# Query, key and value loads in pieces of two heads instead of four, one relu per piece

## The chip, the cores and the metric

The kernel runs on one core of one Trainium2 chip. The metric is the device time of one execution in microseconds (us), lower is better. A core has TensorE (PE, matrix products; PEld is its weight load), VectorE (DVE), ScalarE (ACT), GpSimd (POOL) and SyncE (SP). DMA engines move data between HBM and the core's memory; here GpSimd issues all loads, SyncE nearly all stores and all transposing DMAs.

## The reference

It is an attention without softmax, followed by a gated feed-forward block. There are 8 batches, 12 heads, 448 positions, 64 elements a head; 3584 tokens, a model width of 768 and a hidden width of 1536. All inputs and the output are float32.

```python
scores = scale * np.matmul(q, k.transpose(0, 1, 3, 2))
attn = np.maximum(scores, 0.0) ** 2 / S
attn_out = np.matmul(attn, v)
x = attn_out.transpose(0, 2, 1, 3).reshape(B * S, H * D)
g = x @ w_gate
gelu = 0.5 * g * (1.0 + erf(g * inv_sqrt2))
out = (gelu * (x @ w_val)) @ w_out
```

## The kernel before

All arithmetic on TensorE is in bf16; a load casts from float32 on its way. TensorE works in 64 x 64 tiles, two row groups ("PE0" and "PE1" in the code) running side by side.

**Thirds.** A batch's 12 heads are cut into three *thirds* of four heads (`NM` = 3; a third is written `(b, m)`). A third's queries and keys go into one tile `qk16`, queries on the lower 64 partitions, keys on the upper 64; its values go into `v16`, where either half of the partitions holds four of the seven 64-position chunks. A third has `SC` = 7 units of scores; each unit ends in one relu on ScalarE (line 614, kept as `relus[b, m, 0..6]`), squared afterwards on VectorE. So there are 8 x 3 x 7 = 168 relus.

**From load to scores.** In batches 0 and 1 TensorE transposes `qk16`. From batch 2 on, VectorE copies it into another order (`qkr`, line 382), and SyncE issues two transposing DMAs for each third (line 387, tile `qkT`), each waiting for the one before it. The scores (`sp<-qkT`) read `qkT`; the values (`ff<-attnT,v`) read `v16` and the squared relus. The results of attention (`xT`) then feed the gate and value products, which for part of the hidden width are done as "pairs" with seven products of half the columns (224 instead of 448), and after these the output products, whose results SyncE stores (line 1080).

**Loads.** `load_qk` (line 325) issues one load of queries or keys for the heads `h0` to `h1`, `load_v` (line 342) two loads of values, one for each half of the partitions. Every load is an instruction of GpSimd's queue, which runs strictly in the order of the code: first the weights and batches 0 and 1, then the 18 late thirds (batches 2 to 7), for each its queries and keys, and after them the values of the third before it:

```python
1121    late = [(b, m) for b in range(2, B) for m in range(NM)]
1122    for n, (b, m) in enumerate(late):
1123        for i in range(2):
1124            load_qk(b, i, 4 * m, 4 * m + 4)
1125        for b_, m_ in late[n - 1:n] + (late[n:] if n == len(late) - 1 else []):
1126            load_v(b_, 4 * m_, 4 * m_ + 4)
```

**Pacing.** Late loads are held back so that they come spread over the execution. Queries and keys of the third number n wait for two relus of third n - 3, the values for two relus of third n - 2, which of the seven is in `PACE = 0, 1, 3, 5`. The first two thirds of batch 2 have no such wait for queries and keys:

```python
1274        if (b, m) > (2, 1):
1275            for i, op in enumerate(qk_loads[b, m]):
1276                op.behind.append(relus[(*thirds[n - 3], PACE[i])])
1277        if (b, m) >= (2, 0):
1278            for i, op in enumerate(v_loads[b, m]):
1279                op.behind.append(relus[(*thirds[n - 2], PACE[2 + i])])
```

So the loads that share one third of relus are the queries and keys of a third, then the values of the third before it. A load also waits until its buffer is free: there are two `qk16` (`RING_H`), four `v16` (`RING_V`), four `qkT`.

**Order of the work.** A planner (`run_plan`, line 60) simulates all engines with the costs given in the code and emits the instructions in the order that it finds. TensorE's units, ScalarE's, VectorE's and SyncE's work are chosen by when they are ready; GpSimd's queue is fixed. A load counts in the plan as 0.7 us of GpSimd plus its bytes at a given rate; a regrouping copy is placed 5 us after the last load of its third is taken to have come (`IDLE`, line 376; 2 us in batch 2). What the plan takes for done is only an order: on the chip each instruction waits for what it needs.

Of the kernel before, what the change touches and what calls it, by code (L numbers as in the profile page):

```python
# [196 lines left out]
def kernel(  # L197
# [30 lines left out]
    OGS = d_model // NG  # L228
    WOG = 3
    SB = 2  # L230
    PACE = 0, 1, 3, 5
    FB = 4
    FILL = 30.0
    EARLY = 2
# [39 lines left out]
    HALF = (slice(0, P), slice(P, 2 * P))  # L274
# [21 lines left out]
    qk16, v16 = {}, {}  # L296
    qk_loads, qk_used, v_loads, v_used, t_made, t_used = ({} for _ in range(6))

    def load(nbytes, emit, deps=(), cost=0.7, rate=400e3):
        def paced():  # L300
            ins = emit()
            for d in op.behind:
                tc.add_manual_dep(ins.ins, d.ins.name, SYNC, reason="pace")

        op = Op("POOL", cost, paced, deps)
        op.behind = [*deps]
        arrivals[op] = nbytes / rate
        POOL.append(op)
        return op
# [15 lines left out]
    def load_qk(b, i, h0, h1, deps=()):  # L325

        src = (q, k)[i]
        m, r0 = divmod(h0, 4)

        def tile_of():  # L330
            if (b, m) not in qk16:
                qk16[b, m] = hpool.tile([128, 4, SC * D], bf16, name="qk16", tag="qk16")
            return qk16[b, m][HALF[i], r0:r0 + h1 - h0, :]

        op = load(4 * (h1 - h0) * S * D, lambda: nc.gpsimd.dma_start(
            tile_of(), src[b, h0:h1].rearrange("h (p c) d -> p h (c d)", c=SC)),
            deps, rate=400e3 if b else 300e3)
        qk_loads.setdefault((b, m), []).append(op)
        for pr in range(h0 // 2, h1 // 2):
            head_op[b, pr, i] = op  # L340

    def load_v(b, h0, h1, deps=()):

        m = h0 // 4
        for i in range(2):
            def emit(i=i):
                if (b, m) not in v16:
                    v16[b, m] = qkv.tile([128, 4, VC, D], bf16, name="v16", tag="v16")
                c0 = i * (SC - VC)
                return nc.gpsimd.dma_start(  # L350
                    v16[b, m][HALF[i], :, :, :],
                    v[b, h0:h1].rearrange("h (p c) d -> p h c d", c=SC)[:, :, c0:c0 + VC, :])
            op = load(4 * (h1 - h0) * VC * P * D, emit, deps, rate=400e3 if b else 300e3)
            v_loads.setdefault((b, m), []).append(op)
            for pr in range(h0 // 2, h1 // 2):
                head_op[b, pr, 2 + i] = op
# [298 lines left out]
    relus = {}  # L655
# [464 lines left out]

    late = [(b, m) for b in range(2, B) for m in range(NM)]
    for n, (b, m) in enumerate(late):
        for i in range(2):
            load_qk(b, i, 4 * m, 4 * m + 4)
        for b_, m_ in late[n - 1:n] + (late[n:] if n == len(late) - 1 else []):
            load_v(b_, 4 * m_, 4 * m_ + 4)
    for b, m in late:
        add_dma_transposes(b, m)

# [38 lines left out]
    for at, item in placed:  # L1168
# [4 lines left out]
        else:  # L1173
            _, gr, name, b = item
# [93 lines left out]
    thirds = [(b, m) for b in range(B) for m in range(NM)]  # L1268
# [4 lines left out]
    for n, (b, m) in enumerate(thirds):  # L1273
        if (b, m) > (2, 1):
            for i, op in enumerate(qk_loads[b, m]):
                op.behind.append(relus[(*thirds[n - 3], PACE[i])])
        if (b, m) >= (2, 0):
            for i, op in enumerate(v_loads[b, m]):
                op.behind.append(relus[(*thirds[n - 2], PACE[2 + i])])
        for op in (*qk_loads[b, m], *v_loads[b, m]):  # L1280
            op.deps += op.behind
    for new, old in zip(duos[RING_A:], duos):
# [45 lines left out]
```

## Time and profile before

| | |
|---|---|
| three runs | 417.73 us median (412.75, 417.73, 418.99) |
| the profiled execution | 418.04 us, span of its instructions 416.3 us |
| granted TensorE clock | 0.995 of full speed, mean over the span |
| busy | TensorE 396.3, VectorE 285.5, ScalarE 245.2, GpSimd 74.7 us |
| loads | q and k 50, v 48, weights 16; all on GpSimd |
| DMA | 75287 packets, 45.00 MB |

The profile shows one execution. "Busy" is the time in which an engine ran at least one instruction; a wait is the idle time ahead of an instruction, put down to what released it, and "issue" is idle time for which the profile shows no releaser. A row of the timeline gives the start, the length, the engine, the line of the code, the operation, what it writes and reads, and in brackets the idle time ahead of it. DMA rates count the bytes on the bf16 side. q0 is the queue of GpSimd's loads, q1 that of SyncE's stores and transposes, q8 is named "instruction".

### The profile page before, as it was taken

The numbers are of one execution on the slowest core, as the hardware profiler recorded it, in microseconds if no ns is written. First come the engines' busy times: TensorE is split into PE (matmuls) and PEld (weight loads), VectorE is DVE, ScalarE is ACT, GpSimd is POOL, SyncE is SP. The second block draws the span as 40 slices with busy tenths as digits, with TensorE's granted clock in tenths as the row PEclk, the third lists the DMA queues.
The fourth block names the chain that finished last, engine by engine and source line by source line (L and its number), as shares of the span: only waits on it lengthen the run. The fifth ranks groups of instructions, "written<-read, shape, count | busy, mean of one in ns | idle before, by whom it ended". The sixth has DMA issues, their size and how long they took to land.

```text
span 416.3 us, 21002 instructions
## 1 busy us (share of the span) xinstructions
PE 396.3 (95%) x9703; PEld 358.8 (86%) x9706; DVE 285.5 (69%) x498; ACT 245.2 (59%) x367; POOL 74.7 (18%) x120
## 2 busy tenths in 40 slices
PE   7999999989998999997999989999999999999995
PEld 3556888879997899997889879898999999999994
DVE  3967797866886788665777767768766785655352
ACT  5958573456777667584556756777555856343230
POOL 7755410211121121111111112112101000000000
PEclk9999999999999999998999999999999999999999
DMA  8999997979799957895736956868633400050005
GB/s 109 192 200 197 198 211 120 117 102 173 84 150 186 135 77 95 126 194 43 104 61 90 168 110 80 97 90 143 99 60 66 117 6 2 3 136 23 3 22 134
DMA packets 75287, 45.00 MB, mean 108 GB/s; under 512 B 36160, under 2 KB 71744, under 8 KB 75200
## 3 DMA queue, kind: packets, MB, share of 16 engines
q0 software_dynamic: 37152, 24.39, 44.2%
q1 hardware_dynamic: 37888, 19.08, 24.9%
q8 instruction: 76, 1.25, 1.2%
q10 hardware_dynamic: 160, 0.20, 0.2%
q14 instruction: 11, 0.09, 0.1%
HBM read 48.76 MB, written 11.01 MB: 144 GB/s over the span
## 4 chain that ended last, share of the span: by engine, by line
PE 95%; issue 3%; ACT 1%; DVE 0%; ACTq 0%
PE ff L280 83%; PE sp L280 8%; PE ff L468 1%; PE ff L1264 1%; PE sp L547 1%; PE ff L547 0%; ACT gel L821 0%; ACT rl L614 0%; PE ff L510 0%; ACT qkT L518 0%; ACT osb L1066 0%; DVE warm L266 0%; DVE table L269 0%; ACTq L821 0%
## 5 line engine op out<-in xcount | busy, mean ns | idle before, releaser
L280 PE MATMUL ff<-xT,wg 64*64 64x448 bf16 (+1 forms) x2304 | 207.8, 322 | 1.4 <-issue 1.4
L614 ACT ACTIVATE rl<-sp 128x896 bf16<-128x896 f32 x168 | 152.0, 922 | 74.6 <-PE sp L280 53.3
L280 PE MATMUL ff<-xT,wv 64*64 64x448 bf16 x1632 | 177.2, 351 | 2.1 <-issue 2.1
L280 PEld LDWEIGHTS <-wv 64*64 64x64 bf16 x2304 | 131.2, 107 | 14.8 <-issue 7.1
L280 PEld LDWEIGHTS <-wg 64*64 64x64 bf16 x2304 | 129.7, 107 | 11.3 <-issue 4.0
L626 DVE TENSOR_TENSOR attnT<-rl 128x1792 bf16<-128x1792 bf16 (+1 forms) x98 | 92.2, 952 | 8.0 <-ACT rl L614 7.6
L280 PE MATMUL ff<-attnT,v 64*64 64x448 bf16 (+1 forms) x768 | 84.3, 328 | 0.1
L280 PEld LDWEIGHTS <-s 64*64 64x64 bf16 x1344 | 77.3, 107 | 1.1 <-issue 0.6
L280 PE MATMUL sp<-qkT 64*64 64x448 bf16 (+1 forms) x768 | 74.8, 329 | 1.7 <-ACT gel L821 0.6
L902 DVE TENSOR_TENSOR uT<-gel,ff 128x448 bf16<-128x448 bf16 x68 | 42.2, 620 | 33.7 <-PE ff L280 27.1
L280 PEld LDWEIGHTS <-uT 64*64 64x64 bf16 x1008 | 63.4, 107 | 0.8
L280 PE MATMUL ff<-wo,s 64*64 64x384 bf16 x672 | 59.8, 323 | 1.9 <-issue 1.9
L280 PE MATMUL ff<-wo,uT 64*64 64x384 bf16 x672 | 60.6, 322 | 0.0
L897 ACT ACTIVATE gel<-ff 128x448 bf16<-128x448 f32 x68 | 37.0, 545 | 36.0 <-PE ff L280 35.3
L350 POOL DMA_DIRECT2D v<-in_v_dram x48 | 30.3, 636 | 125.0 <-ACT rl L614 113.0
L280 PE MATMUL ff<-wt,s 64*64 64x384 bf16 x672 | 52.1, 323 | 0.0
L280 PEld LDWEIGHTS <-ws 64*64 64x64 bf16 x1008 | 48.0, 108 | 2.7 <-issue 2.3
L280 PEld LDWEIGHTS <-v 64*64 64x64 bf16 x768 | 46.4, 107 | 4.0 <-issue 1.5
L1066 ACT COPY osb<-ff 128x384 f32<-128x384 f32 x56 | 26.7, 479 | 36.2 <-PE ff L280 33.5
L686 DVE TENSOR_SCALAR xT<-ff 128x448 bf16<-128x448 f32 x46 | 28.7, 623 | 24.5 <-PE ff L280 24.2
L280 PE MATMUL ff<-ts,wv 64*64 64x224 bf16 x672 | 40.5, 259 | 4.0 <-issue 4.0
L280 PEld LDWEIGHTS <-qkT 64*64 64x64 bf16 x768 | 36.0, 106 | 8.7 <-issue 5.1
(52 smaller groups left out, 343.3 us busy)
## 6 DMA issues: line engine op xcount, KB each, us to landing
out_dram<-osb SPq DMA_DIRECT2D x54, 192.0 KB, 4.1
v<-in_v_dram POOLq DMA_DIRECT2D x48, 128.0 KB, 3.9
qk<-in_q_dram POOLq DMA_DIRECT2D x23, 224.0 KB, 5.1
qk<-in_k_dram POOLq DMA_DIRECT2D x23, 224.0 KB, 5.9
wg<-in_moe_w_gate_dram POOLq DMA_DIRECT2D x6, 384.0 KB, 10.3
wv<-in_moe_w_val_dram POOLq DMA_DIRECT2D x6, 384.0 KB, 11.4
wo<-in_moe_w_out_dram POOLq DMA_DIRECT2D x4, 576.0 KB, 14.8
qkT<-qkr SPq DMA_TRANSPOSE x36, 5.0
```

What stands on the lines that cost most here:

```text
L280: return nc.tensor.matmul(o, lhsT, rhs, start=start, stop=stop, skip_group_check=onto, tile_position=(P * row, P * col))
L350: return nc.gpsimd.dma_start(v16[b, m][HALF[i], :, :, :], v[b, h0:h1].rearrange("h (p c) d -> p h c d", c=SC)[:, :, c0:c0 + VC, :])
L468: nc.tensor.matmul(t[:, :], warm[:, 0:128], warm[:, :], start=True, stop=True)
L547: nc.tensor.transpose(t[HALF[j], c, :], src[:, 2 * r + j, c, :], ident[:, :], tile_position=(0, P * j))
L614: relu.ins = nc.scalar.activation(duo["rl"][:, u % 2, :, :], box[0][:, :, 0:S], AF.Relu).ins
L626: nc.vector.tensor_tensor(a[:, part], duo["rl"][:, part], duo["rl"][:, part], op=ALU.mult)
L686: nc.vector.tensor_scalar_mul(xT[b][:, pr, :], box[0][:, 0:S], scalar1=out_scale)
L897: nc.scalar.activation(gel[b, fc][:, :], box[0][:, 0:S], AF.Gelu)
L902: u_op[b, fc].ins = nc.vector.tensor_tensor(uT[b][:, fc, :], gel.pop((b, fc))[:, :], box[0][:, 0:S], op=ALU.mult).ins
L1066: ins = nc.scalar.copy(o, box[0][:, 0:OGS])
L1264: nc.tensor.matmul(t[HALF[j], :], warm[:, HALF[j]], warm[:, :], start=True, stop=True, tile_position=(0, P * j))
```

## The change

From batch 2 on, every load of queries, keys or values covers two heads instead of four, so each is cut into two and the 18 late thirds have eight loads each instead of four. The order within a third is queries and keys of its first two heads, queries and keys of its second two, and later the values of two heads, then of the other two. `PACE` has an entry for each of the eight: the first two share relu 0, the others have a relu of their own, 1 to 6. Tiles, buffers, transposes, matmuls and bytes stay as they are; the planner sees the new loads with their costs.

```diff
-    PACE = 0, 1, 3, 5
+    PACE = 0, 0, 1, 2, 3, 4, 5, 6
...
                 return nc.gpsimd.dma_start(
-                    v16[b, m][HALF[i], :, :, :],
+                    v16[b, m][HALF[i], h0 - 4 * m:h1 - 4 * m, :, :],
                     v[b, h0:h1].rearrange("h (p c) d -> p h c d", c=SC)[:, :, c0:c0 + VC, :])
...
     late = [(b, m) for b in range(2, B) for m in range(NM)]
     for n, (b, m) in enumerate(late):
-        for i in range(2):
-            load_qk(b, i, 4 * m, 4 * m + 4)
+        for h0 in (4 * m, 4 * m + 2):
+            for i in range(2):
+                load_qk(b, i, h0, h0 + 2)
         for b_, m_ in late[n - 1:n] + (late[n:] if n == len(late) - 1 else []):
-            load_v(b_, 4 * m_, 4 * m_ + 4)
+            for h0 in (4 * m_, 4 * m_ + 2):
+                load_v(b_, h0, h0 + 2)
...
             for i, op in enumerate(v_loads[b, m]):
-                op.behind.append(relus[(*thirds[n - 2], PACE[2 + i])])
+                op.behind.append(relus[(*thirds[n - 2], PACE[4 + i])])
```

## The prediction

> **What bounds the kernel now.** I read the page first, for the engine that fills the span and for the chain that ended last.
>
> ```profile
> PE 396.3 (95%) x9703; PEld 358.8 (86%) x9706; DVE 285.5 (69%) x498; ACT 245.2 (59%) x367; POOL 74.7 (18%) x120
> q0 software_dynamic: 37152, 24.39, 44.2%
> q8 instruction: 76, 1.25, 1.2%
> PE 95%; issue 3%; ACT 1%; DVE 0%; ACTq 0%
> ```
>
> TensorE is busy for 95% of the span, and the chain lies on it for 95%. A load can matter only by making TensorE wait: directly, because its data come late, or indirectly. So I went on to the waits of TensorE, and to its timeline at the longest of them.
>
> ```profile
> PE ff L280 <- issue: 11.3, 9, 2.1
> 85.23 0.32 PE L280 MATMUL ff<-wo,s 64*64 64x384 bf16 x1 [1.88 <-issue]
> 133.39 0.29 PE L280 MATMUL ff<-ts,wv 64*64 64x224 bf16 x4 [2.00 <-issue]
> 189.48 0.38 PE L280 MATMUL ff<-xT,wv 64*64 64x448 bf16 x2 [2.15 <-issue]
> 243.18 0.28 PE L280 MATMUL ff<-xT,ws 64*64 64x224 bf16 x2 [1.83 <-issue]
> ```
>
> No wait of weight stands on a load, a copy or a transpose. 11.3 us in nine waits are "issue": TensorE waited for nothing that its semaphores show. The rows lie about 50 us apart, where a new batch's pair products start (224 columns, so the most instructions per us). The cause is in the DMA view of the stretches before and after 187.1 us, beside the wait that ends at 189.48 (queue: packets, MB, share of 16 engines):
>
> ```profile
> q1 hardware_dynamic: 1233, 0.65, 69.2%
> q0 software_dynamic: 480, 0.40, 54.8%
> ...
> q1 hardware_dynamic: 779, 0.20, 96.5%
> q8 instruction: 1, 0.02, 2.5%
> ```
>
> The first two rows are 182.0 to 187.1 us, the last two 187.1 to 189.5. Queue q8 carries 76 packets in all, 1.25 MB, so 16 KB each, while TensorE has 9703 + 9706 instructions: 255 for each packet. I read q8 as TensorE's own instruction stream. Between 182.0 and 187.1 none of it moved, while loads (q0) and stores and transposes (q1) together took 124% of the 16 engines; TensorE then stood until 189.48. So the path has one soft spot that loads can touch: **instruction blocks that queue behind data**. That reading is an inference from these rows.
>
> A long wait also costs clock. The row of windows gives TensorE's busy time, then the other engines', the granted clock, and the DMA share:
>
> ```profile
> 187.00:189.00 2.00, 0.33 (x12) 0.09 (x2) 0.73 (x2) 0.80 (x1) 0.00 (x0) 1.00 1.18 107
> 191.00:193.00 2.00, 2.00 (x34) 1.74 (x30) 2.00 (x4) 0.92 (x1) 0.00 (x0) 0.50 0.39 49
> 187.00:194.00 7.00, 4.85 (x96) 4.32 (x90) 3.61 (x8) 1.72 (x2) 0.61 (x1) 0.76 0.52 54
> ```
>
> After the 2.15 us wait the clock fell to 0.50; over 7 us it averaged 0.76, a loss of 7 x 0.24 = 1.7 us. The waits of 1.83 to 2.00 us have no such loss on the page.
>
> The Trainium skill ("TensorE: Matmul & The Clock Gate", Part 1) puts this down to a free-running 3.4 us activity window, whose idle verdict halves the clock for at least one more. The trace agrees in size: 1.7 us lost at half clock is 3.4 us of it. By that rule the phase decides too, not the length alone.
>
> **What is edited.** Third by third (four heads, seven relus) the queue of GpSimd now stands like this, in the third with relus at 177 to 197 us:
>
> ```profile
> 178.66 0.61 POOL L335 DMA_DIRECT2D qk<-in_q_dram  x1 [4.83 <-DVE osb L1064]
> 182.05 0.61 POOL L335 DMA_DIRECT2D qk<-in_k_dram  x1 [2.78 <-ACT rl L614]
> 189.21 0.61 POOL L350 DMA_DIRECT2D v<-in_v_dram  x1 [6.55 <-issue]
> 195.56 0.61 POOL L350 DMA_DIRECT2D v<-in_v_dram  x1 [5.74 <-ACT rl L614]
> ...
> 177.45 0.92 ACT L614 ACTIVATE rl<-sp 128x896 bf16<-128x896 f32 x1
> 180.83 0.92 ACT L614 ACTIVATE rl<-sp 128x896 bf16<-128x896 f32 x1
> 185.14 0.94 ACT L614 ACTIVATE rl<-sp 128x896 bf16<-128x896 f32 x1
> 186.89 0.92 ACT L614 ACTIVATE rl<-sp 128x896 bf16<-128x896 f32 x1 [0.32 <-PE sp L280]
> 191.86 0.92 ACT L614 ACTIVATE rl<-sp 128x896 bf16<-128x896 f32 x1 [4.05 <-PE sp L280]
> ```
>
> Query load behind relu 0, key load behind relu 1, the value halves behind 3 and 5, each about 0.3 us after its relu's end (the first value load 1.4 us). After the edit there are eight: q and k of the first two heads behind relu 0, q of the second two behind 1, its k behind 2, the value pieces behind 3, 4, 5 and 6. The same bytes move; in this third the last quarter of q and k moves from 182.05 to about 186.4, the first value load splits over about 188 and 193.
>
> **Issue on GpSimd.** 18 late thirds x 4 more loads = 72, at 0.61 us each: 44 us of GpSimd, 74.7 becoming 119 of 416. A third's eight take 4.9 us in a stretch of 11 to 20 us. What hides them:
>
> ```profile
> POOL v L350 <- ACT rl L614: 113.0, 32, 11.1
> POOL qk L335 <- ACT rl L614: 70.5, 27, 11.4
> ```
>
> It waits 184 us for these very relus. Cost 0. Only later loads are queued behind a waiting load, in order of their relus, and the last of a third (relu 6) precedes the next third's relu 0. With no cover, 44 us would only delay loads that are far ahead of use, as the next step shows.
>
> **Arrival.** DMA issues: KB, median us to landing:
>
> ```profile
> qk<-in_k_dram POOLq DMA_DIRECT2D x23, 224.0 KB, 5.9
> qk<-in_k_dram POOLq DMA_DIRECT2D x2, 112.0 KB, 2.8
> ```
>
> A tile is whole one relu later (1.75 to 4.3 us in the rows above), but its last piece lands 3.1 us sooner after its issue if the first loads' price (2.8) holds, not at all sooner if it doesn't: -1.3 to +4.3 us. I take +1, nearer the common spacing. The regrouping copy on VectorE waits for it, then two transposes on SyncE's queue, then the scores. One third later in the program:
>
> ```profile
> 133.04 0.62 DVE L382 COPY qkr<-qk 128x1792 bf16<-128x1792 bf16 x1
> 133.78 7.76 SPq L387 DMA_TRANSPOSE qkT<-qkr  x3
> qkT<-qkr SPq DMA_TRANSPOSE x36, 5.0
> 162.74 0.40 PE L280 MATMUL sp<-qkT 64*64 64x448 bf16 x4
> ```
>
> The copy at 133.04 belongs to the third whose scores start at 162.74. Its last transpose is issued by 141.5 and lands 5.0 later: 16 us of slack, so +4.3 costs nothing there. VectorE may stand behind a copy that comes late, but the planner places the copy by the loads' relus and moves it too. Values have more: their pieces come two thirds ahead of use. Cost 0, bounded at +2 by the tightest place:
>
> ```profile
> 73.22 2.82 SPq L387 DMA_TRANSPOSE qkT<-qkr  x2
> DMA to landing us min/median/max: 4.4/5.9/10.3
> 85.59 0.47 PE L280 MATMUL sp<-qkT 64*64 64x448 bf16 x4
> ```
>
> These are batch 2's first transposes (landings of 70 to 90 us). The second is issued about 1.4 us before its row ends, at 74.6, took the 10.3 and landed at 84.9, 0.7 us before its scores; a copy 2.7 us late would cost 2.
>
> The Trainium skill ("DMA: Bandwidth & Descriptors", Rules for kernel authors) speaks against pieces: it would have small transfers joined, for each carries a fixed 2 us. By its formula the 72 added loads cost an estimated 144 us of latency. The rows of 2.8 and 5.9 us show much less than that for halves, and no part of it is on TensorE's path.
>
> **Waits of other engines.** The copies await four landings instead of two, and the second pair's values await two of their own: 36 more conditions on TensorE. The view of the tile v shows no idle time of TensorE ahead of its 768 matmuls, so I take 0; at 0.1 us each it would be 3.6.
>
> **Instruction blocks.** This is the one term on the path. The early, DMA-bound stretch gives the rate at which data leave the queues:
>
> ```profile
> 30.00:60.00 30.00, 30.00 (x660) 23.70 (x654) 23.23 (x35) 21.58 (x29) 13.07 (x19) 1.00 1.35 202
> ```
>
> 112 KB at 202 GB/s is 0.57 us, 64 KB is 0.32. In the third above, 112 KB leave the stretch ahead of the block at 187: -0.6. At 133 both value pieces still come ahead of the block (0), at the next wait the second's half leaves (-0.3); at 243 and 85 the same bytes come ahead (0). Sum -0.9. Ends: all nine waits and the clock loss go (-13.0), or each grows by one 112 KB piece (+5.1) and three more halve the clock (+5.1). I take -0.9, since bytes, stores and transposes in those stretches stay.
>
> **Sum.** The profiled execution took 418.04 us around a span of 416.3; 0 + 0 + 0 - 0.9 gives 417.1, and I say **417**. The three runs have a median of 417.73 (412.75 to 418.99); 2% is 8.4 us, about what a measurement of this kernel can tell from no change.
>
> **Rivals.**
>
> *Blocks get through.* If a block waits for whole loads ahead of it, halves spread over seven relus let it in earlier everywhere. For it: every long wait lies in a stretch full of DMA. Against: q1's share there is as large, and q and k of two heads still start together. Half the waits (5.7) and the clock loss (1.7) go: **410.7**; all of it, 405. Chance 0.20.
>
> *Blocks come later and the clock falls.* A piece now comes at nearly every relu, so one is always just ahead of a block at a batch's start. Each of nine waits grows 0.57 (5.1), and those of 1.83, 1.88 and 2.00 pass the 2.15 that halved the clock: 3 x 1.7 = 5.1. **428.2**. It decides from 0.15 to 0.35 us more per wait. For it: the three stand that close. Against: no more bytes. The gate's rule named above would let some of them escape by phase: 425 or so. Chance 0.18.
>
> *Batch 2's start is late.* Eight unpaced pieces at its head push copy and transposes past their scores: +2 to +5, **421**. Against: that stretch is DMA-bound, and the bytes keep their order. Chance 0.07.
>
> *The pieces aren't paced by their relus*, but by something later (the first value load above came 1.4 us late): the loads bunch as before, **418**. Chance 0.05.
>
> **How the numbers follow.** Forecast 417, chance 0.50, its own range 412 to 423. Faster by over 2% (under 409.4) needs the first rival's better half: 0.10, and 0.03 for an order of the planner that happens to miss the stores. Slower by over 2% (over 426.1): most of the second, 0.13, and 0.05 for such an order that hits them. Within 2%: 0.69. Range 408.5 to 427.5, which leaves out the outer halves of both large rivals.
>
> **What would show it.** GpSimd at about 119 us busy with 192 instructions; value loads of 64 KB, q and k of 112 KB landing in about 3 us; no wait of TensorE on a copy, a transpose or a load; "issue" waits between 9 and 13 us, at the starts of batches 2 to 5. Wrong, if those waits sum below 6 or above 16, if the clock shows 0.5 in more than one place, or if VectorE waits for a load ahead of a regrouping copy and TensorE behind it.

## The result, and the profile after

The changed kernel took 412.63 us in the median of its runs (409.96 to 415.91), the kernel before 416.83 us (412.75 to 422.17), 20 runs each on the same chip. The ratio is 0.9917, with a 95% interval of 0.9888 to 0.9947: **3.5 us less** (2.2 to 4.7), within 2% of no change, and plainly not zero. The result lies inside the range, between the forecast (417) and the first rival (410.7). Executions more than 1.5% above the fastest of their kernel are left out of all ratios here, though not of the medians; the profiled executions of two experiments (the doubled loads, and the pieces at the old relus) are such ones, so what is read from their traces is read for its kind, not for its exact size.

The profiled execution of the changed kernel took 415.91 us, the longest of its 20. Its page answers to the lines of before as follows (engines; TensorE's clock in 40 slices; queues; the chain; issues of loads with KB and median us to landing):

```profile
span 414.1 us, 21156 instructions
PE 399.2 (96%) x9706; PEld 360.5 (87%) x9706; DVE 285.0 (69%) x498; ACT 245.0 (59%) x367; POOL 115.5 (28%) x192
PEclk9999999989999899999999999999999999999999
q0 software_dynamic: 38304, 24.39, 44.6%
q8 instruction: 76, 1.25, 1.2%
PE 96%; issue 2%; DMA 1%; ACT 0%; POOL 0%; POOLq 0%
v<-in_v_dram POOLq DMA_DIRECT2D x72, 64.0 KB, 3.0
qk<-in_q_dram POOLq DMA_DIRECT2D x38, 112.0 KB, 4.1
qk<-in_k_dram POOLq DMA_DIRECT2D x38, 112.0 KB, 4.3
```

GpSimd has 72 instructions more and 40.8 us more of busy time, the same 24.39 MB move, and the chain still lies on TensorE. VectorE and ScalarE are as before. "Issue" has lost one of its three per cent. TensorE's waits (total us, times, longest), and the four long ones in the timeline:

```profile
PE ff L280 <- issue: 8.2, 5, 2.8
...
PE ff L510 <- DMA qk<-in_k_dram: 0.2, 1, 0.2
...
85.17 0.32 PE L280 MATMUL ff<-wo,s 64*64 64x384 bf16 x1 [2.75 <-issue]
135.55 0.39 PE L280 MATMUL ff<-ts,wv 64*64 64x224 bf16 x8 [2.55 <-issue]
187.61 0.38 PE L280 MATMUL ff<-xT,wg 64*64 64x448 bf16 x2 [1.65 <-issue]
242.17 0.28 PE L280 MATMUL ff<-xT,ws 64*64 64x224 bf16 x2 [1.01 <-issue]
```

The waits stand where they stood before (85, 133, 189, 243 us), and their sum is 8.2 instead of 11.3 us. What has gone in this execution are short ones, five being left of nine: the four long ones together are unchanged, 7.96 against 7.86 us. Two are longer here than before, 2.75 for 1.88 and 2.55 for 2.00, and after each of these the clock drops, as the windows show (TensorE's busy time first, then the other engines', then the granted clock, DMA share and GB/s):

```profile
85.17:90.17 5.00, 5.00 (x96) 4.95 (x99) 1.48 (x3) 2.01 (x3) 1.19 (x2) 0.66 0.45 76
135.00:141.00 6.00, 5.45 (x120) 5.00 (x124) 1.09 (x2) 2.42 (x4) 0.52 (x1) 0.72 0.82 122
```

These two cost 5 x 0.34 + 6 x 0.28 = 3.4 us, about the 3.3 us by which this execution is above the median of its kernel. One execution of a kernel whose waits come and go by microseconds is a sample, not the kernel: the sections below therefore rest on the ratios of many runs, and use the traces for the mechanism.

### The profile page after: what moved, and what is told of

It reads as the page before. It is cut to its first block, busy times and chain, and to the rows that moved or that the text cites. A ratio compares the mean times of both kernels' runs of the same rounds, so it can differ in the third digit from the quotient of the medians.

```text
span 414.1 us, 21156 instructions
## 1 busy us (share of the span) xinstructions
PE 399.2 (96%) x9706; PEld 360.5 (87%) x9706; DVE 285.0 (69%) x498; ACT 245.0 (59%) x367; POOL 115.5 (28%) x192
## 3 DMA queue, kind: packets, MB, share of 16 engines
q0 software_dynamic: 38304, 24.39, 44.6%
q8 instruction: 76, 1.25, 1.2%
## 4 chain that ended last, share of the span: by engine, by line
PE 96%; issue 2%; DMA 1%; ACT 0%; POOL 0%; POOLq 0%
PE ff L280 84%; PE sp L280 9%; PE ff L468 1%; PE ff L547 1%; DMA qk<-in_k_dram 1%; PE sp L547 1%; PE ff L510 0%; ACT qkT L518 0%; ACT osb L1066 0%; POOL qk L335 0%; POOLq L1314 0%
## 5 line engine op out<-in xcount | busy, mean ns | idle before, releaser
L280 PEld LDWEIGHTS <-wv 64*64 64x64 bf16 x2304 | 133.1, 108 | 11.5 <-issue 4.0
L280 PE MATMUL ff<-attnT,v 64*64 64x448 bf16 (+1 forms) x768 | 85.8, 329 | 0.2
L350 POOL DMA_DIRECT2D v<-in_v_dram x84 | 50.4, 607 | 108.6 <-ACT rl L614 102.5
L280 PE MATMUL sp<-qkT 64*64 64x448 bf16 (+1 forms) x768 | 77.0, 334 | 0.6 <-ACT qkT L518 0.6
L280 PE MATMUL ff<-wo,s 64*64 64x384 bf16 x672 | 61.1, 326 | 2.8 <-issue 2.8
L280 PEld LDWEIGHTS <-ws 64*64 64x64 bf16 x1008 | 49.6, 108 | 2.2 <-issue 1.8
L280 PE MATMUL ff<-ts,wv 64*64 64x224 bf16 x672 | 42.5, 261 | 2.5 <-issue 2.5
## 6 DMA issues: line engine op xcount, KB each, us to landing
qk<-in_q_dram POOLq DMA_DIRECT2D x38, 112.0 KB, 4.1
qk<-in_k_dram POOLq DMA_DIRECT2D x38, 112.0 KB, 4.3
wv<-in_moe_w_val_dram POOLq DMA_DIRECT2D x6, 384.0 KB, 11.3
```

The costliest lines, as they stand in the source:

```text
L280: return nc.tensor.matmul(o, lhsT, rhs, start=start, stop=stop, skip_group_check=onto, tile_position=(P * row, P * col))
L350: return nc.gpsimd.dma_start(v16[b, m][HALF[i], h0 - 4 * m:h1 - 4 * m, :, :], v[b, h0:h1].rearrange("h (p c) d -> p h c d", c=SC)[:, :, c0 ...
```

## The experiments

Three sets, each on one chip, each kernel timed between runs of the kernel before on that chip. Median of the kernel before: 414.86 us (35 runs), 416.63 (23) and 416.39 (29).

### Loads or order of the work?

The change does two things at once: it alters when the loads travel, and it gives the planner other loads, so that the order of TensorE's, VectorE's and SyncE's work comes out differently. Two kernels take these apart. The first has the order of before, the planner seeing two loads for each pair, while the pieces and their relus are those of the changed kernel (extra pieces are issued by entries that cost the plan nothing; one that issues nothing keeps the place and the cost of the old second load):

```diff
-    PACE = 0, 1, 3, 5
+    PACE_QK, PACE_V = (0, 0, 1, 1, 2), (3, 4, 5, 6)
...
+        ops = [load(whole, lambda: piece(0, 0)), load(0, lambda: piece(1, 0), cost=0.0),
+               load(0, lambda: piece(0, 2), cost=0.0), load(whole, lambda: None),
+               load(0, lambda: piece(1, 2), cost=0.0)]
```

> Order of the instructions on TensorE, VectorE, ScalarE and SyncE as before, late loads as in the changed kernel (pieces of two heads, relus 0,0,1,2,3,4,5,6). Theory 'spread': the gain comes from what the loads do on the chip, so this kernel has nearly all of it: ratio to before 0.990 to 0.995, issue waits of TensorE some 3 us shorter. Theory 'order': the gain comes from the planner's other order from TensorE instruction 8809 of 19414 on (about 193 us), so the ratio is 0.998 to 1.002.

Measured: 413.71 us, ratio 0.9978 (0.9946 to 1.0011), between the two ranges that were expected and nearer to that of 'order'. The second kernel has the order of the changed one, and whole loads at relus 0, 1, 3 and 5 as before:

```diff
+        ops = [load(half, lambda: whole(0)), load(half, lambda: None),
+               load(half, lambda: whole(1)), load(half, lambda: None)]
```

> The converse: order of the instructions as in the changed kernel, late loads as before (four heads, relus 0,1,3,5). 'Spread': ratio 0.998 to 1.002. 'Order': 0.990 to 0.995.

Measured: 415.09 us, 1.0014 (0.9981 to 1.0047). So the new order alone gains nothing. That the pieces alone gain was not shown here, as their interval reaches 1. Both were therefore run again, beside the changed kernel itself, in the third set:

> The changed kernel beside the two crossings, all on one chip, since its two ratios (0.992, 0.990) and those of the crossings (0.998, 1.001) came from different sets of runs. 'Spread': 0.990 to 0.996, equal to the old order with pieces within its interval. 'Both': the pieces pay only with the new order, 0.990 to 0.993 here and 0.997 to 1.000 for the old order with pieces.

> Old order, spread pieces, once more. 'Spread': as the changed kernel within 0.003. 'Both': at least 0.004 above it.

> New order, whole loads, once more. 'Spread' and 'both': 0.998 to 1.003. 'Order': as the changed kernel, 0.990 to 0.996.

Measured: the changed kernel 413.72 us, 0.9936 (0.99 to 0.9972); old order with pieces 412.70, 0.9922 (0.9886 to 0.9959); new order with whole loads 417.25, 1.0023 (0.9987 to 1.006). On one chip, then, the pieces without the new order gain what the whole change gains, and the new order without the pieces nothing. The order of the work is not the cause. The first set's 0.9978 is weaker than the third's 0.9922, though the intervals overlap; on that chip the kernel before was itself 1.5 us faster, and why is open.

### Which batches?

Pieces in batch 2 alone, and from batch 3 on alone:

```diff
+        step = 2 if b == 2 else 4      # the other kernel: b > 2
+        for h0 in range(4 * m, 4 * m + 4, step):
...
+    PACE, PACE4 = (0, 0, 1, 2, 3, 4, 5, 6), (0, 1, 3, 5)
```

> Order as before, pieces in batch 2 alone, whose loads meet the end of the weights' loads (46 to 85 us). Before to after, TensorE gains 2.1 us between 67 and 82 us in the profiled executions, with the same order of instructions. 'Start': that gain is real and of these loads: ratio 0.995 (0.993 to 0.997), no issue wait at 69 us. 'Spread' over all batches alike: 3 of 18 thirds, ratio 0.998 to 1.000. 'Order': 1.000.

> Order as in the changed kernel, batch 2 in whole loads, batches 3 to 7 in pieces. 'Start': ratio 0.996 to 1.000, the issue wait at 69 us is back. 'Spread' over all batches alike: 0.992 to 0.995. 'Order': 0.990 to 0.995, as in the kernel with whole loads and the new order.

Measured: 414.53 us, 0.999 (0.9952 to 1.0027), and 413.50, 0.9971 (0.9935 to 1.0007). The first fits 'spread' and 'order', the second only 'start', so the two do not agree on a theory. The kernel before has a wait of 0.97 us at the start of batch 2; the changed kernel's first trace and the one with pieces in batch 2 do not have it, the one with pieces from batch 3 on has it again. First the row of before, then that of the latter:

```profile
69.93 0.44 PE L280 MATMUL ff<-xT,wg 64*64 64x224 bf16 x9 [0.97 <-issue]
```

```profile
71.20 0.44 PE L280 MATMUL ff<-xT,wg 64*64 64x224 bf16 x9 [0.97 <-issue]
```

That would put this wait down to batch 2's loads, but the changed kernel's trace in the second set, with pieces in batch 2, has it as well:

```profile
69.91 0.29 PE L280 MATMUL ff<-xT,wg 64*64 64x224 bf16 x4 [0.79 <-issue]
```

So that is not shown. By the lower ends of the two intervals batch 2 alone gains at most 2.0 us and the others alone at most 2.7, and both intervals hold no change as well. On the same chip the pieces in all batches, in the old order, gained at most 2.2 us (0.9946). How the gain divides stays open.

### Smaller pieces, or pieces spread out?

The second set has the changed kernel again, and the same pieces in pairs at the four relus of before:

```diff
-    PACE = 0, 0, 1, 2, 3, 4, 5, 6
+    PACE = 0, 0, 1, 1, 3, 3, 5, 5
```

> The changed kernel once more, beside the kernel before and the three others of this set, so that all are read on one chip. 'Spread' (the pieces' traffic on the chip, any order): ratio 0.992 to 0.997, since the four crossings of order and loads gave 0.998 and 0.997 with pieces, 1.001 and 0.999 without or in batch 2 alone. 'Order': no different from the new order with whole loads, 1.000 to 1.003.

> Pieces of two heads, but two and two behind the relus of before (0,0,1,1 and 3,3,5,5); TensorE's order as before. If it is the size of a piece that helps (a block of instructions gets in between two loads), ratio 0.994 to 0.998, as with the spread pieces. If it is the spreading over more relus, 1.000, for the queue gets the same bytes at the same relus as before.

Measured: 412.00 us, 0.9901 (0.9865 to 0.9936), against 415.50, 0.9987 (0.9952 to 1.0022). The intervals do not overlap (0.9936 against 0.9952). Halving the loads is worth nothing that can be measured; **giving each piece a relu of its own is what gains**, on this chip by a narrow margin between the intervals.

### The disputed mechanism by itself: more traffic, and less

If TensorE's instruction blocks (queue q8, 16 KB each) wait behind the loads' data, more data at the same places must lengthen the "issue" waits, and none there must remove them. In the first kernel every late load from batch 3 on is followed, at the same relu, by a second read of the same rows (three heads of four for queries and keys) into a spare tile that nobody reads; the order of the work is that of before.

```diff
+            ins = [nc.gpsimd.dma_start(tile_of(), rows)]
+            if b >= 3:
+                ins.append(nc.gpsimd.dma_start(spare[HALF[i], :, :], rows[:, 0:3, :]))
```

> The kernel before, same order on all engines, with every load of batches 3 to 7 followed at the same relu by a second read of the same bytes (three heads of four for q and k) into a spare tile that nobody reads; the output is the same. Theory 'blocks behind data': TensorE's own instruction blocks wait behind the loads, so the issue waits at the batch starts from 130 us on grow from 7 to 13 us or more, with half-clock windows behind them: ratio 1.010 to 1.030, and no wait of TensorE on a load. Theory 'arrival': loads matter through late data; then waits on copies, transposes or values appear. Theory 'loads don't matter there' (stores and transposes alone hold the blocks): 1.000 to 1.004.

Measured: 438.25 us (433.43 to 440.54), ratio 1.0469 (1.04 to 1.0538), more than the 1.010 to 1.030 expected: 19.5 us lost for 9.1 MB more (54.10 against 45.00 on the two pages). From its page, waits and timeline:

```profile
q0 software_dynamic: 51552, 33.48, 59.4%
PEclk8899999999999799998999969999999999999999
PE ff L282 <- issue: 20.6, 12, 4.9
PE sp L282 <- issue: 2.0, 1, 2.0
PE sp L282 <- DMA qkT<-qkr: 1.8, 2, 1.1
...
141.70 0.59 PE L282 MATMUL ff<-ts,wv 64*64 64x224 bf16 x8 [4.30 <-issue]
198.44 0.58 PE L282 MATMUL ff<-xT,wg 64*64 64x448 bf16 x2 [4.03 <-issue]
255.34 0.40 PE L282 MATMUL ff<-ts,wv 64*64 64x224 bf16 x2 [4.85 <-issue]
```

The long waits at the starts of batches 3 to 5 are about twice as long (4.30, 4.03 and 4.85 for 2.00, 2.15 and 1.83 us), the first line's sum is 20.6 instead of 11.3 us, and the clock falls after each of the three (the 7, the 8 and the 6 from the 14th slice on, each 11 us long). The wait at the start of batch 2, whose loads were not doubled, did not grow: 1.61 us at 87.87, for 1.88. The wait for the transposes is new as well, 1.8 us: not all of the loss is instruction blocks.

The second kernel is the changed one with its loads kept out of the starts of batches 3, 4, 5 and 6, where TensorE has the most instructions per us. Queries and keys that fell there wait for later relus of the same third, values for the first relu of the next third; one third of batch 2's values is also moved:

```diff
+    QUIET = {(3, 0): (6, 6, 6, 6), (4, 1): (4, 4, 5, 6), (5, 1): (4, 4, 5, 6), (6, 1): (4, 4, 5, 6)}
...
+                op.behind.append(relus[(*thirds[n - 3], QUIET.get(thirds[n - 3], PACE)[i])])
...
+                if thirds[n - 2] in QUIET or (b, m) == (2, 1):
+                    op.behind.append(relus[(*thirds[n - 1], 0)])
```

> The changed kernel with the loads kept out of the stretches in which TensorE stood: those that shared relus with third (3,0) wait for its relu 6, those of (4,1), (5,1) and (6,1) for relus 4 to 6, and the values of these thirds and of (2,1) for relu 0 of the third after. Same pieces and bytes; the planner's order moves. 'Blocks behind data': the issue waits at 83, 133, 187 and 240 us fall to half, ratio to before 0.985 to 0.990, below the changed kernel's. 'Stores and transposes alone': as the changed kernel, 0.992 to 0.997. If the loads now come too late, TensorE or VectorE waits for copies or values and it is over 1.000.

Measured: 407.61 us (407.00 to 410.67), ratio 0.9798 (0.9755 to 0.9841): **faster than both kernels**, and than the 0.985 to 0.990 expected. Its waits, and its windows around the start of batch 3:

```profile
PE ff L281 <- issue: 3.0, 4, 1.1
...
120.00:134.00 14.00, 14.00 (x434) 13.51 (x429) 10.99 (x17) 11.60 (x19) 0.88 (x2) 1.00 0.76 173
```

The kernel before in the same window:

```profile
120.00:134.00 14.00, 11.99 (x363) 11.56 (x356) 11.53 (x18) 9.86 (x16) 3.10 (x5) 1.00 1.02 153
```

TensorE had 2.0 us idle in 14 and now has none; it gets through 434 matmuls instead of 363. What is on the queues there helps to tell the cause from mere load on the DMA engines. Packets, MB and share of 16 engines, at 124 to 130 us in the new kernel:

```profile
q1 hardware_dynamic: 1523, 1.41, 91.4%
q8 instruction: 1, 0.02, 1.2%
q0 software_dynamic: 17, 0.01, 1.0%
```

and at 126 to 131 us in the kernel before, ahead of its wait of 2.00 us at 133:

```profile
q0 software_dynamic: 485, 0.41, 56.8%
q1 hardware_dynamic: 760, 0.55, 53.8%
q8 instruction: 1, 0.02, 1.3%
```

Stores and transposes alone, at 91% of the engines, let the blocks through without a wait. Loads and stores together, at 111%, do not.

Last, the same pacing with the *whole* loads of before, in its own planned order:

```diff
+    QUIET = {(3, 0): (6, 6), (4, 1): (4, 5), (5, 1): (4, 5), (6, 1): (4, 5)}
```

> The kernel before with whole loads, kept out of the same stretches as in the quiet kernel with pieces (0.980). If what counts is only that no load lies ahead of an instruction block at a batch's start, the size of the pieces doesn't matter: ratio 0.980 to 0.985, issue waits of 3 to 5 us. If pieces are needed too: 0.987 to 0.995.

Measured: 408.30 us (405.96 to 410.36), 0.9832 (0.9776 to 0.9887). Its waits:

```profile
PE ff L281 <- issue: 2.8, 6, 1.0
```

No piece is needed for the larger gain. The loads of before, moved away from four batch starts, gain 7 us, and pieces with the same pacing gain no more that can be measured (0.9832 and 0.9798, intervals that overlap). My reading is that the pieces' 3.5 us are a part of it, got by thinning the loads instead of moving them.

This kernel also tells whether it is the 111% that counts, rather than the loads in it. At 126 to 131 us it has no load on the queues, and stores and transposes alone take 112%; TensorE has no idle time (queues, then the window):

```profile
q1 hardware_dynamic: 1354, 1.03, 112.0%
q8 instruction: 2, 0.03, 2.8%
126.00:131.00 5.00, 5.00 (x185) 4.94 (x179) 3.67 (x6) 4.71 (x10) 0.00 (x0) 1.00 1.15 213
```

At the same share of the engines, then, it was in these executions the loads among the data that made TensorE wait there. What no run separates is the order of the work: both kernels with moved loads have an order of their own, planned anew. That the waits went where the loads went speaks for the loads.

### The delay of the blocks in all kernels

From each trace I took the 49 packets of q8 numbered 9 to 57, counted from 0 (71 to 322 us in the kernel before, so from batch 2 to the last loads) and compared the start of packet n with that of TensorE's instruction number 185 + 256 n, matmuls, weight loads and the entries of its sequencer counted. The zero is arbitrary, since 185 is only the place where a packet with free engines starts at about that instruction; the differences are what counts. The traces of some executions lack up to three matmuls, which shifts this by less than 0.1 us.

| loads | mean delay, us | ratio measured |
|---|---|---|
| doubled | 2.85 | 1.047 |
| whole, relus 0, 1, 3, 5: before; new order, twice | 1.80; 1.75, 1.65 | 1; 1.001, 1.002 |
| pieces, relus 0, 0, 1, 1, 3, 3, 5, 5 | 1.78 | 0.999 |
| pieces in batch 2 alone | 1.75 | 0.999 |
| pieces from batch 3 on alone | 1.57 | 0.997 |
| pieces spread: changed kernel, three times | 1.45, 1.58, 1.41 | 0.992, 0.990, 0.994 |
| pieces spread, old order, twice | 1.51, 1.55 | 0.998, 0.992 |
| out of the batch starts: pieces; whole | 1.38; 1.25 | 0.980; 0.983 |

The delay orders the kernels nearly as their times do. The last row falls out of line: 1.38 is hardly less than the 1.41 above it, and its time is 1.4% better. My reading is that a block's delay costs only where TensorE runs through its 256 instructions quickly, and that the last two kernels take it from just these places. Splitting the blocks bears this out. Where TensorE needs less than 4.5 us for the next 256 instructions, waits left out (15 to 18 of the 49 blocks), the mean delay is 2.52 us in the kernel before, 1.88, 2.23 and 1.95 in the three traces of the changed kernel, and 1.70 (pieces) and 1.24 (whole) with the loads out of the batch starts; at the other blocks it is 1.42, then 1.26, 1.30 and 1.18, then 1.21 and 1.25.

The same count shows that these waits are waits for instruction blocks, which the prediction had only inferred. The 14 traces have 100 "issue" waits of TensorE between 60 and 330 us. **Every one of them ends at the same place of a block of 256**, within one instruction: at its number 193 or 194, counted from 0 (190 or 191 in the traces that lack three matmuls), and 2.2 to 3.3 us after a packet of q8 has started.

## Why the prediction was right, and where it was not

**Issue on GpSimd** (cost 0): right. 115.5 us and 192 instructions, where about 119 and 192 were said. The waits of GpSimd for relus fell and still leave cover:

```profile
POOL v L350 <- ACT rl L614: 102.5, 62, 9.5
POOL qk L335 <- ACT rl L614: 60.9, 44, 9.3
```

163 us instead of 184. Pieces at the old relus, with the same 72 instructions, cost nothing either (0.9987).

**Arrival** (cost 0): right in the sum, a little off in its parts. Pieces of queries and keys landed 4.1 and 4.3 us after their issue, not the 2.8 of the first loads in the quiet start, so the last key piece gains 1.6 us on the 5.9 of a whole load rather than 3.1. No wait of TensorE on a late load, copy or transpose is among its waits; the 0.2 us on a key load stands at line 510, which belongs to the first batches. The rival of a late batch 2 did not come up, since TensorE did not wait for a transpose. **Waits of other engines** (0): nothing of it showed.

**The rule of the Trainium skill on joining small transfers** ("DMA: Bandwidth & Descriptors", Rules for kernel authors) would have had 72 loads more cost latency. The runs at the old relus bound that cost at 0.2% (0.9987, upper end 1.0022).

**Instruction blocks** (-0.9): **this is the step that failed**, in size and in its counting, not in its mechanism. It credited a block only with bytes that leave the stretch ahead of it, and let the clock stand. Measured was -3.5 us (ratio 0.9917; 0.9901 and 0.9936 in the other sets, so 2.7 to 4.1), about four times as much. That the time still lies within the range says little for the step, since the range was wide enough to hold the first rival's 410.7 as well. Place by place it cannot be judged from one execution: the wait at 189 was to lose 0.6 us and lost 0.5, but that at 243 was to stay and lost 0.8, and those at 85 and 133 were to stay and grew by 0.9 and 0.6. The wait after 133, of 0.87 us, was to lose 0.3 and is gone, but so it is with whole loads in the new order. The three traces of the changed kernel have 2.75, 1.88 and 1.33 us at 85, 2.55, 4.07 and 2.94 at 133, 1.65, 0.94 and 0.87 at 189, 1.01, 0.46 and 0.73 at 243: shorter than before at the last two places, longer at the second. At 243 it is shorter with whole loads in the new order too (0.46 and 0.18). What the step overlooked is what the first rival said: a load that is spread over the relus lets the blocks in earlier at every boundary, whether or not it leaves a given stretch. The delay fell from about 1.73 us (mean of the three traces with whole loads) to 1.50 (mean of the five with spread pieces) over all 49 blocks. In the profiled executions the "issue" waits, foreseen between 9 and 13 us, were 11.3, 10.0 and 9.9 with whole loads, and 8.2, 9.9, 6.4, 5.6 and 8.6 with spread ones, by the first row of each trace's waits, of which these are two:

```profile
PE ff L280 <- issue: 6.4, 5, 2.9
```

(the changed kernel in the third set) and

```profile
PE ff L280 <- issue: 9.9, 7, 2.4
```

(the new order with whole loads, same chip). That is 10.4 to 7.7 on average, 2.7 us of the 3.5, with a scatter as large: pieces in batch 2 alone had 6.8, pieces from batch 3 on 10.7, pieces at the old relus 12.5. The granted clock accounts for little: the time lost to it, span times one minus the mean clock, was 2.0, 2.3 and 2.1 us for the kernel before in the three sets (32, 20 and 26 runs), and 1.8, 1.5 and 1.9 for the changed one (20 runs of the result, 12 and 10 of the second and third set), some 0.4 us less on average. Together 3.1, near the 3.5, with a sample of one execution for each wait.

**The first rival** ("Blocks get through", 410.7) had the mechanism and about twice the size: it took half of all waits and all of the clock loss. With a chance of 0.20 it was held too low. The argument used against it, that q1's share in those stretches is as large as q0's, falls with the 91.4% and the 112.0% of q1 at which no block made TensorE wait.

**The second rival** ("Blocks come later and the clock falls") did happen in part: the two waits of 2.75 and 2.55 us halved the clock twice, which by the prediction's own words ("if the clock shows 0.5 in more than one place") counts against it. In the other two traces of the changed kernel the clock was halved once, after the waits of 4.07 and 2.94 us. Over all runs the mean loss of clock is still smaller than before. **That pieces are not paced by their relus** is out: the row of waits above is for relus, and pieces at other relus gave another time.

The Trainium skill ("Runtime: NRT & Kernel Launch", Instruction fetch mechanics) says that instructions are streamed in 16 KiB blocks of 256 by the sequencer's own DMA queue, and that crossing a block's border is mostly hidden. The trace agrees with the size (76 packets, 1.25 MB, 255 instructions each). It does not agree that this stays hidden where loads and stores fill the engines: 11.3 us of waits before, 20.6 with the loads doubled, 3.0 with the loads out of the way.

**What stays open.** Why one and the same wait is 1.9 us in one execution and 2.7 or 0.2 in another was not traced; how the gain divides over the batches, the two kernels for it did not tell; no kernel moved loads out of the batch starts in the order of before; and no kernel spread *whole* loads over more relus without also moving them out of the batch starts.

## What to carry to other kernels

When the bounding engine shows idle time with no releaser in its densest stretch, look at the instruction queue in the DMA view: if each wait ends 2 to 3 us after one of its packets starts, and always at the same place of the engine's count of instructions, while loads and stores fill the DMA engines, the engine is starved of instructions by data that nobody needs yet. Then pace the early loads by place, not by size: here moving them out of the dense stretches gained 1.7 and 2.0%, spreading them evenly 0.8%, cutting them smaller nothing. A cost or gain counted as "bytes that leave the stretch ahead of the wait" misses most of what spreading does; doubling and removing the traffic measures the mechanism at both ends.

## What the hardware showed that was not expected

**Full DMA engines alone did not make TensorE wait; it mattered whose data filled them.** With stores and transposes at 91.4% and loads at 1.0% TensorE had no idle time in 14 us, and at 112.0% without a load none in 5; with 53.8% and 56.8% it stood for 2.00 us. They are not without effect: in the kernel before, the block due at 373 us, with no load near and stores and transposes at 73% of the engines in the 4 us ahead, came 2.3 us late by the measure of the table, though TensorE did not wait for it.

**The length of a wait does not decide alone whether the clock is halved.** In the kernel with pieces from batch 3 on, a wait of 1.97 us did it:

```profile
139.68 0.28 PE L280 MATMUL ff<-ts,wv 64*64 64x224 bf16 x2 [1.97 <-issue]
...
139.70:144.70 5.00, 5.00 (x110) 4.59 (x114) 3.12 (x5) 1.84 (x2) 1.18 (x2) 0.66 0.75 121
```

and in the kernel with the new order and whole loads one of 2.04 us did not:

```profile
187.12 0.38 PE L280 MATMUL ff<-xT,wg 64*64 64x448 bf16 x2 [2.04 <-issue]
...
187.10:192.10 5.00, 4.48 (x144) 4.10 (x148) 2.25 (x3) 3.20 (x5) 0.00 (x0) 1.00 0.99 164
```

The prediction's threshold of 2.15 us was therefore no threshold. What decides can be read from the records of the granted clock, which every trace has: in each trace the clock changes only at multiples of 3.41 us from its first change. Cut at these times, the stretch from 60 to 330 us of the 14 traces has 14 windows at full clock in which TensorE ran no matmul for 1.97 us or more, and half clock followed each of them; it followed none with 1.83 us or less. The wait of 1.97 us lay within one window, that of 2.04 us across two, with 1.77 and 0.27 us. The Trainium skill ("TensorE: Matmul & The Clock Gate", Part 1) has a window of about 3.4 us that runs free of the kernel, and the traces agree with that. Its table asks for an idle window before the clock is halved; here 1.97 us of 3.41 were enough.
